# Reordering, re-laying and rewriting the tail of a one-token attention and gated-MLP kernel

## The chip, the cores and the metric

The kernel runs on one core of a Trainium2 chip. The time is device microseconds of one execution, the median of several. The profile is a trace of one execution; its span (first to last recorded instruction) is about 2 us shorter than the time (685.6 against 687.48 us in the profiled run of the kernel before).

Engines in the profile's lines: PE is TensorE's matmul, PEld its weight load, DVE is VectorE, ACT is ScalarE, POOL is GpSimd, SPq is the SyncE queue that issues the DMA transfers.

## The reference, cut to what matters

One decoding step for 4 sequences. The caches hold 32 heads of 4096 keys and values of 128 numbers in bf16: 134 MB each, and all of it is read once.

```python
mod = (silu(c) @ w_mod)                       # six modulation vectors of 512
h = layernorm(x) * (1 + ca) + sa
x = x + ga * attention(h, k_cache, v_cache, wq, wo)
h = layernorm(x) * (1 + cb) + sb
z = gelu_tanh(h @ w_in)                       # 4 x 1792, split in z1 and z2 of 896
g = w_sp * layernorm(z2) + b_sp               # w_sp and b_sp are one number each here
x = x + gb * ((z1 * g) @ w_out)
```

## The kernel before: the parts that matter

The caches are read in 32 tiles each (4 heads of one sequence, 4 MB), on one DMA queue, in the order K, V, K, V; the last key tile comes in two pieces and the last value tile in four. `w_in` and `w_out` are issued behind the last value tile. Scores of a tile are a VectorE product and 16 PE matmuls for each half; `fold` and `softmax` turn them into probabilities, `values` multiplies them with the value tile (128 matmuls of 4 columns), `project` normalises and, after every fourth tile, multiplies with `wo`.

```python
def load_v(i):
    return load(A_v_cache, i, "vt", 4 if i == len(quads) - 1 else 1)   # number of equal pieces

for i in range(NQ + 1):                    # NQ = 32
    ...                                    # loads, query projections, scores(i, 0)
    if i > 1:
        project(i - 2)
    if i > 0:
        fold(i - 1, 1)
        softmax(i - 1)
    if i < NQ:
        scores(i, 1)
        fold(i, 0)
    if i > 0:
        values(i - 1, 0)
        values(i - 1, 1)
project(NQ - 1)
...
nc.sync.dma_start(out=win, in_=B_w_in.rearrange("(j p) n -> p j n", p=P))
nc.sync.dma_start(out=wout, in_=B_w_out.rearrange("(p j) n -> p j n", j=JF))
...                                        # x1, second layernorm -> h2T
for s in range(2):
    for jf in range(JF):
        for j in range(J):
            nc.tensor.matmul(
                z_ps[:, s, jf, :], lhsT=win[:, j, s * FH + jf:(s + 1) * FH:JF],  # every 7th column
                rhs=h2T[:, j, :], start=(j == 0), stop=(j == J - 1),
            )
...   # GELU as copy, 3 steps, exp on ScalarE, add, reciprocal, two products: z1, z2
mean, rstd = ln_stats(post, psum_s, z2b, mean_f, JF, "ln3")
...   # gt = (z2 - mean) * rstd * w_sp + b_sp; uT = gt * z1
...   # y_ps = uT times w_out, 28 matmuls of 4 columns; y = y_ps * modT[5]; yo = y + x1
```

## Time and profile before

| | before |
|---|---|
| time, median | 687.32 us (687.23 to 687.5, 4 runs) |
| span of the profile | 685.6 us |
| read from HBM | 282.73 MB |
| next-to-last value tile landed | 654.28 us |
| span left after that | 31.3 us |

The page's slice view of the kernel before cuts the span in 40 slices of 17 us; a digit is a tenth of busy time (9 is 90% or more), the row GB/s is what the DMA engines moved.

```profile
span 685.6 us, 12370 instructions
...
PEclk9985887777777777777787777777777767776965
DMA  9999999999999999999999999999999999999980
GB/s 368 427 425 429 427 425 425 429 427 431 435 414 428 432 435 426 427 426 427 432 421 430 426 431 435 418 431 429 434 435 420 428 431 435 427 425 418 431 327 12
...
```

The DMA engines are busy from the first slice to the 38th. So the time up to there is set by the transfers, and the change, which leaves the loop as it is, can only shorten the last 30 us.

The chain of waits of the kernel before, from the issue of the next-to-last value tile (columns: start in us, length in us, what):

```profile
...
620.90 33.38 DMA vt<-in_A_v_cache_dram
...
654.32 3.42 PE zo_ps L283 x128
...
657.76 0.19 DVE rz L294
...
658.15 0.60 DVE S L246
...
660.15 0.59 ACT P L267 x2
...
661.97 0.59 ACT P L267 x2
...
663.19 3.43 PE zo_ps L283 x128
...
667.07 0.30 PE attn_ps L302 x6
667.37 1.47 issue
668.84 0.44 PE attn_ps L302 x10
...
672.61 3.13 PE zf_ps L375 x56
...
675.76 0.23 DVE z L380
...
678.35 0.69 PE small L132 x2
...
681.07 0.90 PE y_ps L408 x28
...
682.20 0.21 DVE yo L415
...
```

Two things are to be seen. The last softmax (658.15 to 662.5) begins only after the values of tile 30 (654.32 to 657.74) and their normalisation (`rz`, `oT`), though its scores were done at 653.1: `project(30)` stands before `fold(31, 1)` in VectorE's order. And from 667.37 to 668.84 PE waits for nothing that the profile can name ("issue"), between the sixth and the seventh of 16 matmuls. From 672.61 on `w_in`, the GELU steps, the statistics and `w_out` follow each other with no overlap.

Lines of the timeline of the kernel before (start, length, engine, line, operation, operands, count, and in brackets the idle time before it and what ended it):

```profile
...
667.07 0.30 PE L302 MATMUL attn_ps<-oT,wo_g 128*128 128x4 bf16 x6 [0.47 <-DVE oT L295]
...
668.84 0.42 PE L302 MATMUL attn_ps<-oT,wo_g 128*128 128x4 bf16 x10 [1.47 <-issue]
...
672.58 3.06 PEld L375 LDWEIGHTS <-wt 128*128 128x128 bf16 x56 [2.07 <-issue]
672.61 3.12 PE L375 MATMUL zf_ps<-h2T,wt 128*128 128x4 bf16 x56 [1.96 <-DVE h2T L369]
...
```

The 56 weight loads for `w_in` take 3.06 us, and PE follows at that pace: 56 ns a matmul. The DMA records of the trace show a packet of 16384 bytes on the instruction queue from 666.23 to 667.31 us.

### The profile page before, as it was taken

How to read it: one execution, taken by the hardware profiler on the slowest of the kernel's cores; microseconds unless marked ns; L12 is line 12 of the kernel's file. 1: busy time of each engine (PE TensorE's matmuls, PEld its weight loads, DVE VectorE, ACT ScalarE, POOL GpSimd, SP SyncE). 2: the span in 40 equal slices, each digit the busy share in tenths (PEclk: the TensorE clock that was granted, in tenths of full speed). 3: DMA queues.
4: the chain of work that ended last, by engine and by line, in shares of the span. 5: the costliest groups of instructions: out<-in, count | busy, mean ns of one | idle time of the engine just before them, and what ended most of it. 6: DMA issues, size and time to landing. Idle time of an engine off the chain costs nothing.

```text
span 685.6 us, 12370 instructions
## 1 busy us (share of the span) xinstructions
PE 428.9 (63%) x5696; PEld 249.4 (36%) x5696; DVE 370.7 (54%) x407; ACT 82.7 (12%) x277; POOL 3.6 (1%) x17
## 2 busy tenths in 40 slices
PE   2675856765666666557766455676655577665853
PEld 1241433432334323334433233443333344333443
DVE  2835555466652666445566645546664455665713
ACT  1012101111110111101111100111110011111110
POOL 2000000000000000000000000000000000000000
PEclk9985887777777777777787777777777767776965
DMA  9999999999999999999999999999999999999980
GB/s 368 427 425 429 427 425 425 429 427 431 435 414 428 432 435 426 427 426 427 432 421 430 426 431 435 418 431 429 434 435 420 428 431 435 427 425 418 431 327 12
DMA packets 16963, 283.52 MB, mean 414 GB/s; under 512 B 1416, under 2 KB 6032, under 8 KB 8208
## 3 DMA queue, kind: packets, MB, share of 16 engines
q1 hardware_dynamic: 16832, 282.73, 96.9%
q8 instruction: 44, 0.72, 0.4%
q14 instruction: 7, 0.06, 0.0%
q0 software_dynamic: 64, 0.00, 0.0%
q10 hardware_dynamic: 16, 0.01, 0.0%
HBM read 282.73 MB, written 0.00 MB: 412 GB/s over the span
## 4 chain that ended last, share of the span: by engine, by line
DMA 62%; DVE 21%; PE 15%; issue 1%; ACT 1%; SPq 0%; DVEq 0%; ACTq 0%
DMA kt<-in_A_k_cache_dram 57%; DVE kt L232 17%; PE s_ps L237 12%; DMA vt<-in_A_v_cache_dram 5%; PE zo_ps L283 1%; DVE S L246 1%; DVE mx L254 1%; PE zf_ps L375 0%; DVE mT L256 0%; DVE nm L264 0%; DVE hm L258 0%; ACT P L267 0%; DVE hb L260 0%; DVE oT L295 0%; PE attn_ps L302 0%
## 5 line engine op out<-in xcount | busy, mean ns | idle before, releaser
L237 PE MATMUL s_ps<-kt,ident 128*128 128x512 bf16 x1024 | 294.2, 453 | 224.2 <-DVE kt L232 224.2
L232 DVE TENSOR_TENSOR kt<-kt,qbc 128x8192 bf16<-128x8192 bf16 x64 | 281.8, 4404 | 259.1 <-DMA kt<-in_A_k_cache_dram 259.1
L237 PEld LDWEIGHTS <-ident 128*128 128x128 bf16 x1024 | 115.3, 113 | 389.6 <-issue 247.9
L267 ACT ACTIVATE P<-S,nm 32x128 bf16<-32x128 f32 x128 | 73.9, 577 | 537.3 <-DVE nm L264 534.7
L283 PEld LDWEIGHTS <-vt 128*128 128x128 bf16 x4096 | 108.7, 97 | 1.2 <-DMA vt<-in_A_v_cache_dram 1.2
L283 PE MATMUL zo_ps<-P,vt 128*128 128x4 bf16 x4096 | 108.1, 164 | 1.1 <-DMA vt<-in_A_v_cache_dram 1.1
L246 DVE TENSOR_REDUCE S<-s_ps 128x64 f32<-128x512 f32 x64 | 43.6, 682 | 1.4 <-PE s_ps L237 1.3
L267 ACT ACTIVATION_READ_ACCUMULATOR P<-S,nm 32x1 f32 x128 | 32.1, 251 | 0.0
L278 PEld LDWEIGHTS zo_ps<-rs,ones_f 128*128 128x128 f32 x64 | 12.3, 194 | 9.4 <-ACT P L267 5.0
L185 PE MATMUL big<-wt,hbc 128*32 128x384 bf16 (+1 forms) x128 | 12.2, 525 | 4.2 <-ACT qbc L330 3.7
L294 DVE RECIPROCAL rz<-zo_ps 128x4 f32<-128x4 f32 x32 | 5.6, 175 | 14.3 <-PE zo_ps L283 14.3
L278 PE MATMUL zo_ps<-rs,ones_f 128*128 128x4 f32 x64 | 9.3, 216 | 4.9 <-ACT P L267 4.9
L185 PEld LDWEIGHTS <-hbc 128*32 128x32 bf16 x192 | 6.1, 124 | 13.5 <-issue 10.1
L254 DVE TENSOR_REDUCE mx<-S 128x1 f32<-128x128 f32 x32 | 9.2, 286 | 1.3
L264 DVE STREAM_TRANSPOSE nm<-hb 128x32 f32<-128x32 f32 x32 | 6.8, 212 | 3.2
L330 ACT CAST qbc<-big 128x384 bf16<-128x384 f32 (+1 forms) x8 | 4.3, 532 | 32.7 <-PE big L185 32.7
L256 DVE STREAM_TRANSPOSE mT<-mx 128x32 f32<-128x32 f32 x32 | 6.8, 212 | 1.1
L258 DVE TENSOR_REDUCE hm<-mT 128x1 f32<-128x32 f32 x32 | 5.9, 186 | 1.1
L260 DVE TENSOR_SCALAR hb<-hm 128x32 f32<-128x32 f32 x32 | 5.8, 181 | 1.1
L295 DVE TENSOR_TENSOR oT<-zo_ps,rz 128x4 bf16<-128x4 f32 x32 | 5.4, 168 | 1.1
L302 PEld LDWEIGHTS <-wo_g 128*128 128x128 bf16 x128 | 4.5, 97 | 3.7 <-issue 2.1
L302 PE MATMUL attn_ps<-oT,wo_g 128*128 128x4 bf16 x128 | 4.5, 165 | 1.9 <-issue 1.5
(83 smaller groups left out, 39.9 us busy)
## 6 DMA issues: line engine op xcount, KB each, us to landing
kt<-in_A_k_cache_dram SPq DMA_DIRECT2D x31, 4096.0 KB, 25.6
vt<-in_A_v_cache_dram SPq DMA_DIRECT2D x31, 4096.0 KB, 33.4
wo_g<-in_A_wo_dram SPq DMA_DIRECT2D x8, 512.0 KB, 25.4
kt<-in_A_k_cache_dram SPq DMA_DIRECT2D x2, 2048.0 KB, 23.9
vt<-in_A_v_cache_dram SPq DMA_DIRECT2D x4, 1024.0 KB, 17.3
wt<-in_A_wq_dram SPq DMA_DIRECT2D x1, 3584.0 KB
wt<-in_w_mod_dram SPq DMA_DIRECT2D x1, 2048.0 KB, 36.8
wt<-in_B_w_in_dram SPq DMA_DIRECT2D x1, 1792.0 KB
```

The source lines that it names most:

```text
L185: nc.tensor.matmul(qp[hl * R:(hl + 1) * R, col:col + n], lhsT=hbc[:, j, b, :], rhs=wv[:, g0 - hl0:g0 - hl0 + n, hl, :], start=(j == 0), st ...
L232: nc.vector.tensor_tensor(out=kt, in0=kt, in1=q[:, None, :].to_broadcast([P, HT, DH]), op=ALU.mult,)
L237: nc.tensor.matmul(ps, lhsT=ident, rhs=kt[:, :, cc * DC:(cc + 1) * DC], start=(cc == 0), stop=(cc == DH // DC - 1),)
L246: nc.vector.tensor_reduce(out=st["S", i][:, half * HT:(half + 1) * HT], in_=st.pop(("s", i, half)), axis=AX.X, op=ALU.add,)
L254: nc.vector.tensor_reduce(out=mx[:, 0:1], in_=S, axis=AX.X, op=ALU.max)
L256: nc.vector.transpose(out=mT, in_=mx)
L258: nc.vector.tensor_reduce(out=hm, in_=mT, axis=AX.X, op=ALU.max)
L264: nc.vector.transpose(out=nm, in_=hb)
L267: nc.scalar.activation(out=P4[rows, :, hl], in_=S[rows, :], func=AF.Exp, bias=nm[rows, 0:1], scale=att_scale, accum_out=rs4[rows, hl:hl + 1],)
L278: nc.tensor.matmul(st["z", i], lhsT=ones_f, rhs=rs4s[i % NB], start=True, stop=True,)
L283: nc.tensor.matmul(o_ps, lhsT=st["v", i][:, n, :], rhs=P4[:, n, :], start=(n == 0), stop=(n == NT - 1),)
L302: nc.tensor.matmul(attn_ps[:, jo, :], lhsT=wo_g[:, hl, jo * P:(jo + 1) * P], rhs=oT[:, hl, :], start=(g == 0 and hl == 0 and jo == 0), sto ...
```

## The change

The intent: shorten the tail. (1) For the last tile, fold and softmax go ahead of the projection of tile 30. (2) The last value tile comes in 1/2, 1/4, 1/8, 1/8, so that little work is left behind the last piece. (3) The hidden features are numbered so that the 128 columns of a `w_in` weight load are contiguous; `w_out` is then read in rows of 1024 bytes rather than 7168. (4) GELU becomes one ScalarE function, read straight from PSUM, with table loads placed by hand; the z2 half of `w_in` is multiplied first, into a PSUM tile of its own, so that its GELU can start while PE works on the z1 half. (5) `w_out` multiplies the pair (z1\*z2, z1), before mean and rstd of z2 are known; they are applied to the result, since (z1\*((z2 - mean)\*rstd\*w + b)) @ w_out is w\*rstd\*((z1\*z2) @ w_out - mean\*(z1 @ w_out)) + b\*(z1 @ w_out). (6) The tile name `small` in PSUM gets one buffer instead of two. (7) A helper `keep_busy` is added, but emits nothing.

```diff
-        return load(A_v_cache, i, "vt", 4 if i == len(quads) - 1 else 1)
+        return load(A_v_cache, i, "vt", (2, 4, 8, 8) if i == len(quads) - 1 else (1,))
...
-        ps = psum.tile([P, 2, n, B], F32, name="small", bufs=2)       # and in four more places
+        ps = psum.tile([P, 2, n, B], F32, name="small", bufs=1)
...
-            if i > 1:
+            if 1 < i < NQ:
                 project(i - 2)
             if i > 0:
                 fold(i - 1, 1)
                 softmax(i - 1)
+            if i == NQ:
+                project(i - 2)
...
-        nc.sync.dma_start(out=wout, in_=B_w_out.rearrange("(p j) n -> p j n", j=JF))
+        nc.sync.dma_start(out=wout, in_=B_w_out.rearrange("(j p) n -> p j n", p=P))
...
         mean, rstd = ln_stats(post, psum_s, x1b, mean_d, J, "ln2")
+        nc.scalar.preload_act_table_set("gelu_apprx_tanh_and_others")
+        keep_busy(32)                                                  # empty
...
-        for s in range(2):
+        z_ps = [psum.tile([P, JF, B], F32, name=f"zf{s}_ps") for s in range(2)]
+        for s in (1, 0):
...
-                        z_ps[:, s, jf, :], lhsT=win[:, j, s * FH + jf:(s + 1) * FH:JF],
+                        z_ps[s][:, jf, :], lhsT=win[:, j, s * FH + jf * P:s * FH + (jf + 1) * P],
...
-        (nine steps of GELU; mean, rstd; gt; uT)
+        nc.scalar.activation(out=z2, in_=z_ps[1], func=AF.Gelu_apprx_tanh)
+        u = post.tile([P, JF, 2, B], BF16, name="u")
+        nc.scalar.activation(out=u[:, :, 1, :], in_=z_ps[0], func=AF.Gelu_apprx_tanh)
+        nc.scalar.preload_act_table_set("natural_log_exp_and_others")
+        mean, rstd = ln_stats(post, psum_s, z2b, mean_f, JF, "ln3", lambda:
+            nc.vector.tensor_tensor(out=u[:, :, 0, :], in0=u[:, :, 1, :], in1=z2, op=ALU.mult))
...
-                    y_ps[:, jo, :], lhsT=wout[:, jf, jo * P:(jo + 1) * P], rhs=uT[:, jf, :],
+                    y_ps[:, jo], lhsT=wout[:, jf, jo * P:(jo + 1) * P], rhs=u[:, jf],
...
-        (y = y_ps * modT[5]; yo = y + x1)
+        (yg = y_ps * modT[5]; q = (yg0 - yg1 * mean) * w_sp * rstd; r1 = yg1 * b_sp + x1; yo = q + r1)
```

More of the change, by code (lines that the diff above doesn't have):

```diff
@@ L52 @@
     LN_EPS = 1e-5
-    GK = 0.7978845608028654
     consts = ctx.enter_context(tc.tile_pool(name="consts", bufs=1))
@@ L82, in kv_view, with load @@
         return cache[b, g * NH:(g + 1) * NH].rearrange("h (s n) d -> (h s) (n d)", s=R)
-    def load(cache, i, tag, pieces):
+    def load(cache, i, tag, parts):
         t = kvp.tile([P, NT * DH], BF16, name=tag, bufs=2)
-        w = NT * DH // pieces
-        for k in range(pieces):
-            nc.sync.dma_start(
-                out=t[:, k * w:(k + 1) * w], in_=kv_view(cache, i)[:, k * w:(k + 1) * w],
-            )
+        a = 0
+        for part in parts:
+            b = a + NT * DH // part
+            nc.sync.dma_start(out=t[:, a:b], in_=kv_view(cache, i)[:, a:b])
+            a = b
         return t.rearrange("p (n d) -> p n d", d=DH)
     def load_k(i):
-        return load(A_k_cache, i, "kt", 2 if i == len(quads) - 1 else 1)
+        return load(A_k_cache, i, "kt", (2, 2) if i == len(quads) - 1 else (1,))
     def load_v(i):
-        return load(A_v_cache, i, "vt", 4 if i == len(quads) - 1 else 1)
+        return load(A_v_cache, i, "vt", (2, 4, 8, 8) if i == len(quads) - 1 else (1,))
+    NQ = len(quads)
     ident = consts.tile([P, P], BF16, name="ident")
@@ L111, with keep_busy @@
     nc.vector.memset(eps, LN_EPS)
+    busy_ps = [None]
+    def keep_busy(n):
+        if False:
+            busy_ps[0] = psum_s.tile([P, P], F32, name="busy", bufs=1)
+        for _ in range(0):
+            nc.tensor.matmul(busy_ps[0], lhsT=ident, rhs=ident, start=True, stop=True)
     NB = 3
@@ L126, in bc, with ln_stats @@
         return col[:, None, :].to_broadcast([P, n, B])
-    def ln_stats(pool, psum, buf, ones, n, name):
+    def ln_stats(pool, psum, buf, ones, n, name, meanwhile=None):
         nc.vector.tensor_tensor(out=buf[:, 1], in0=buf[:, 0], in1=buf[:, 0], op=ALU.mult)
-        ps = psum.tile([P, 2, n, B], F32, name="small", bufs=2)
+        ps = psum.tile([P, 2, n, B], F32, name="small", bufs=1)
         nc.tensor.matmul(
@@ L135, in ln_stats @@
         )
+        if meanwhile is not None:
+            meanwhile()
         st = pool.tile([P, 2, B], F32, name=f"st_{name}")
@@ L166, in mod_part @@
     def mod_part(wt, w0, oc):
-        ps = psum_s.tile([P, J, B], F32, name="small", bufs=2)
+        ps = psum_s.tile([P, J, B], F32, name="small", bufs=1)
         for jo in range(J):
@@ L192 @@
     with tc.tile_pool(name="pre", bufs=1) as pre:
-        xc_ps = psum_s.tile([P, J, 2 * B], F32, name="small", bufs=2)
+        xc_ps = psum_s.tile([P, J, 2 * B], F32, name="small", bufs=1)
         for j in range(J):
@@ L219 @@
             nc.scalar.copy(out=qbc[:, b, 0, :], in_=qp[:, b, :])
-        wb_ps = psum_s.tile([P, 2], F32, name="small", bufs=2)
+        wb_ps = psum_s.tile([P, 2], F32, name="small", bufs=1)
         nc.tensor.matmul(wb_ps, lhsT=ones_b, rhs=wb_t, start=True, stop=True)
@@ L282, in values @@
             for n in range(half * HT, (half + 1) * HT):
+                if i == NQ - 1 and n in (NT // 2, 3 * NT // 4, 7 * NT // 8):
+                    keep_busy(NT // 8)
                 nc.tensor.matmul(
@@ L307, in project @@
                         )
-        NQ = len(quads)
         wo_v = A_wo.rearrange("(h p) n -> p h n", p=P)
@@ L369 @@
         nc.vector.tensor_tensor(out=h2T, in0=h2, in1=modT[:, 3], op=ALU.add)
-        z_ps = psum.tile([P, 2, JF, B], F32, name="zf_ps")
-        for s in range(2):
+        z_ps = [psum.tile([P, JF, B], F32, name=f"zf{s}_ps") for s in range(2)]
+        for s in (1, 0):
             for jf in range(JF):
@@ L375 @@
                     nc.tensor.matmul(
-                        z_ps[:, s, jf, :], lhsT=win[:, j, s * FH + jf:(s + 1) * FH:JF],
+                        z_ps[s][:, jf, :], lhsT=win[:, j, s * FH + jf * P:s * FH + (jf + 1) * P],
                         rhs=h2T[:, j, :], start=(j == 0), stop=(j == J - 1),
                     )
-        z = post.tile([P, 2, JF, B], F32, name="z")
-        nc.vector.tensor_copy(out=z, in_=z_ps)
-        zz = post.tile([P, 2, JF, B], F32, name="zz")
-        nc.vector.tensor_tensor(out=zz, in0=z, in1=z, op=ALU.mult)
@@ L383 @@
-        nc.vector.tensor_scalar(
-            out=zz, in0=zz, scalar1=2.0 * GK * 0.044715, scalar2=2.0 * GK,
-            op0=ALU.mult, op1=ALU.add,
-        )
-        nc.vector.tensor_tensor(out=zz, in0=zz, in1=z, op=ALU.mult)
-        nc.scalar.activation(out=zz, in_=zz, func=AF.Exp, scale=-1.0)
-        nc.vector.tensor_scalar_add(out=zz, in0=zz, scalar1=1.0)
-        nc.vector.reciprocal(out=zz, in_=zz)
-        z1 = post.tile([P, JF, B], F32, name="z1")
-        nc.vector.tensor_tensor(out=z1, in0=zz[:, 0], in1=z[:, 0], op=ALU.mult)
+        keep_busy(12)
@@ L393 @@
         z2b = post.tile([P, 2, JF, B], F32, name="z2b")
         z2 = z2b[:, 0]
-        nc.vector.tensor_tensor(out=z2, in0=zz[:, 1], in1=z[:, 1], op=ALU.mult)
-        mean, rstd = ln_stats(post, psum_s, z2b, mean_f, JF, "ln3")
-        gt = post.tile([P, JF, B], F32, name="gt")
-        nc.vector.tensor_tensor(out=gt, in0=z2, in1=bc(mean, JF), op=ALU.subtract)
-        nc.vector.tensor_tensor(out=gt, in0=gt, in1=bc(rstd, JF), op=ALU.mult)
-        nc.vector.tensor_scalar(
-            out=gt, in0=gt, scalar1=wbf[:, 0:1], scalar2=wbf[:, 1:2], op0=ALU.mult, op1=ALU.add,
-        )
@@ L403 @@
-        uT = post.tile([P, JF, B], BF16, name="uT")
-        nc.vector.tensor_tensor(out=uT, in0=gt, in1=z1, op=ALU.mult)
-        y_ps = psum.tile([P, J, B], F32, name="y_ps")
+        nc.scalar.activation(out=z2, in_=z_ps[1], func=AF.Gelu_apprx_tanh)
[4 more added lines that the diff above has]
+            nc.vector.tensor_tensor(out=u[:, :, 0, :], in0=u[:, :, 1, :], in1=z2, op=ALU.mult))
@@ L406 @@
+        y_ps = psum.tile([P, J, 2, B], F32, name="y_ps")
         for jo in range(J):
@@ L408 @@
                 nc.tensor.matmul(
-                    y_ps[:, jo, :], lhsT=wout[:, jf, jo * P:(jo + 1) * P], rhs=uT[:, jf, :],
+                    y_ps[:, jo], lhsT=wout[:, jf, jo * P:(jo + 1) * P], rhs=u[:, jf],
                     start=(jf == 0), stop=(jf == JF - 1),
                 )
-        y = post.tile([P, J, B], F32, name="y")
-        nc.vector.tensor_tensor(out=y, in0=y_ps, in1=modT[:, 5], op=ALU.mult)
+        yg = post.tile([P, J, 2, B], F32, name="yg")
+        nc.vector.tensor_tensor(
+            out=yg, in0=y_ps, in1=modT[:, 5, :, None, :].to_broadcast([P, J, 2, B]), op=ALU.mult,
+        )
+        q = post.tile([P, J, B], F32, name="q")
+        nc.vector.tensor_tensor(out=q, in0=yg[:, :, 1], in1=bc(mean, J), op=ALU.mult)
+        nc.vector.tensor_tensor(out=q, in0=yg[:, :, 0], in1=q, op=ALU.subtract)
+        r1 = post.tile([P, J, B], F32, name="r1")
+        nc.vector.scalar_tensor_tensor(
+            out=r1, in0=yg[:, :, 1], scalar=wbf[:, 1:2], in1=x1, op0=ALU.mult, op1=ALU.add,
+        )
+        nc.vector.scalar_tensor_tensor(
+            out=q, in0=q, scalar=wbf[:, 0:1], in1=bc(rstd, J), op0=ALU.mult, op1=ALU.mult,
+        )
         yo = post.tile([P, B, J], BF16, name="yo")
-        nc.vector.tensor_tensor(out=yo.rearrange("p b j -> p j b"), in0=y, in1=x1, op=ALU.add)
+        nc.vector.tensor_tensor(out=yo.rearrange("p b j -> p j b"), in0=q, in1=r1, op=ALU.add)
         t_ps = psum.tile([J * B, P], F32, name="t_ps")
```

## The prediction

> What bounds the kernel. DMA. The slice view shows DMA at 9 tenths or more for 38 of 40 slices and 425 to 435 GB/s; the page counts 282.73 MB read. The diff alters nothing in the loop over 32 tiles: the instruction order of VectorE, ScalarE and SyncE is the same up to the last tile. So only the tail can pay: from 654.28 us (next-to-last value tile landed) to 685.57 us, 31 us of a 685.6 us span.
>
> The tail before, from the chain of waits and the timeline. 654.32 values of tile 30, 3.42 us on PE; then on VectorE the reciprocal and product of tile 30 and only behind them the last fold and softmax (658.15 to 660.07), since they stand in that order; four exponentials to 662.55; values of tile 31, 663.19 to 666.61; projection with a PE gap of 1.47 us at 667.37 ended by "issue", in which a 16384-byte packet of the instruction queue runs (666.23 to 667.31); second layernorm; 56 matmuls on w_in 672.61 to 675.74 (56 ns each, weight loads 152 ns, against 27 ns and 96 to 104 ns where weights are contiguous); GELU in nine small steps; third layernorm; w_out; output. yo ends at 682.41.
>
> What the change does.
> 1. Fold and softmax of tile 31 go before the projection of tile 30. Its scores end at 653.1, so the exponentials end near 657.7, and PE could go straight on. But the last value tile then binds: by the landings in the trace its quarters land at 656.8, 659.3, 661.8, 664.3. Pieces of 1/2, 1/4, 1/8, 1/8 leave 16 matmuls (0.43 us) after 664.3. Values end at about 664.9, gain 1.7 us, not the 5 us that the order alone promises.
> 2. PE waits for pieces meanwhile[...]. The 1.47 us gap should shrink by about 1 us.
> 3. Contiguous w_in columns: 56 matmuls in about 1.6 us instead of 3.13; the price, 1024-byte rows of w_out, lands perhaps 0.4 us later (46 ns a packet against 275 ns for 7168 bytes) and isn't waited for.
> 4. GELU: seven VectorE steps and an exponential (675.76 to 678.1) become two ScalarE activations of about 0.23 us. The w_out product moves ahead of the layernorm statistics. Two table loads are added, 1.28 us each by the load at the start of this trace. The first hides under h2 and w_in; the second lies between the second GELU and the logarithm and is critical: about 1.3 us[...].
> From the first w_in matmul to the end of yo: 9.80 us before; 4.5 to 6.0 us after, my middle 5.2.
> 5. "small" with one buffer instead of two makes the start serial, about 0.7 us, under the 3.3 us that VectorE waits for the first key tile: free. keep_busy emits nothing.
>
> Sum: 1.7 + 1.0 + (9.8 - 5.2) = 7.3 us. I predict 680.1 us, range 678.6 to 682.0. Faster by over 2% (below 673.6) has chance 0.01, within 2% 0.98, slower 0.01.
>
> Signs. Right if: values of tile 31 wait for DMA and end near 664.9; the "issue" gap in the projection is under 0.7 us; w_in matmuls last under 1.9 us; a table load ends the wait of the last logarithm; yo ends near 675. Wrong if: values(31) still wait for ScalarE; a new instruction-fetch gap opens in w_in or w_out; the table switch costs over 2 us; w_out lands after about 672.5; or the DMA stream itself ends later than 671.

The sum stands, 1.7 + 1.0 + 4.6 = 7.3 us, but the 1.0 us of step 2 stands as the author's estimate. The 9.8 us in the sum is measured; the middle of 5.2 us and the range up to 6.0 are estimates.

## More of the kernel before

PE's granted clock is half of full speed at the end (0.50 in every 5 us stretch from 660 us on).

## The result

| | before | after |
|---|---|---|
| time, median | 687.37 us (687.18 to 687.67, 12 runs) | 678.78 us (678.56 to 678.88, 8 runs) |
| span of the profile | 685.6 | 676.7 |
| next-to-last value tile landed | 654.28 | 654.29 |
| last values end | 666.61 | 664.87 |
| first `w_in` matmul | 672.61 | 669.25 |
| `yo` ends | 682.41 | 673.49 |

The ratio is 0.9874 (95% interval 0.9864 to 0.9884). A ratio here is the mean time of one kernel's fast runs over that of the other's fast runs of the same rounds, so not quite the ratio of the medians quoted. The time fell by 8.6 us or 1.3%, inside the predicted range, 0.2 us from its fast end.

The page's slice view of the kernel after:

```profile
span 676.7 us, 12367 instructions
...
PEclk9985878865678676887667777766787767678885
DMA  9999999999999999999999999999999999999993
GB/s 372 419 417 431 433 429 421 432 431 432 431 421 416 434 431 432 425 426 425 431 431 425 433 432 428 426 423 430 433 430 423 429 427 431 431 426 425 431 410 143
...
```

The loop is as it was; the last slice now still has DMA traffic (143 GB/s), because the kernel ends soon after the last transfer. The chain of waits of the kernel after, in its last part:

```profile
...
644.07 20.16 DMA vt<-in_A_v_cache_dram
...
664.28 0.60 PE zo_ps L297 x16
...
665.34 0.58 PE attn_ps L316 x16
...
669.25 1.63 PE zf_ps L393 x56
670.88 0.51 PE small L142 x2
671.39 0.90 PE y_ps L411 x28
...
672.31 0.20 DVE yg L416
...
673.03 0.25 DVE q L426
...
673.29 0.20 DVE yo L430
...
```

The first line is now the last value tile itself: DMA binds until 664.23 us. Between the last values and `w_in` no piece called "issue" longer than 0.14 us is left. Lines of the timeline of the kernel after, for the groups shown above, the statistics matmul of the third layernorm and the ScalarE operations around it:

```profile
...
665.34 0.56 PE L316 MATMUL attn_ps<-oT,wo_g 128*128 128x4 bf16 x16 [0.48 <-DVE oT L309]
...
669.22 1.58 PEld L393 LDWEIGHTS <-wt 128*128 128x128 bf16 x56 [2.06 <-DMA wt<-in_B_w_in_dram]
669.25 1.63 PE L393 MATMUL zf_ps<-h2T,wt 128*128 128x4 bf16 x56 [1.96 <-DVE h2T L386]
670.17 0.20 ACT L400 ACTIVATE z2b<-zf_ps 128x28 f32<-128x28 f32 x1 [0.39 <-PE zf_ps L393]
...
670.74 0.65 PE L142 MATMUL small<-z2b,mean_f 128*128 128x56 f32 x2
...
671.13 1.28 ACT L405 ACT_TABLE_LOAD   x1
...
672.42 0.30 ACT L157 ACTIVATE rstd_ln<-var_ln,eps 128x4 f32<-128x4 f32 x1
...
```

The 16 projection matmuls come in one run. The 56 `w_in` weight loads take 1.58 us. The GELU of z2 (670.17) starts before the last `w_in` matmul ends (670.88), and the statistics matmul follows without a wait. The second table load ends at 672.41 and the logarithm (L157) starts at 672.42, so the load does hold it up; but its result is ready at 672.95, and the operation that needs it (`q`, 673.03) comes when VectorE gets to it.

By stage the spans differ by 1.7 us up to the end of the last values, 1.6 us from there to the first `w_in` matmul, 5.6 us from there to the end of `yo`, and nothing after it: 8.9 us together.

### The profile page after: what moved, and what is told of

Read it like the earlier page. It is cut to its first block, busy times and chain, and to the rows that moved or that the text cites. A ratio compares the mean times of both kernels' runs of the same rounds, so it can differ in the third digit from the quotient of the medians.

```text
span 676.7 us, 12367 instructions
## 1 busy us (share of the span) xinstructions
PE 429.6 (63%) x5696; PEld 248.3 (37%) x5696; DVE 369.2 (55%) x400; ACT 85.4 (13%) x280; POOL 3.5 (1%) x17
## 4 chain that ended last, share of the span: by engine, by line
DMA 63%; DVE 25%; PE 11%; issue 1%; SPq 0%; ACT 0%; DVEq 0%
DMA kt<-in_A_k_cache_dram 60%; DVE kt L244 20%; PE s_ps L249 9%; DMA vt<-in_A_v_cache_dram 3%; DVE S L258 1%; DVE mx L266 1%; PE zo_ps L297 1%; DVE mT L268 0%; DVE nm L276 0%; DVE hm L270 0%; DVE hb L272 0%; DVE oT L309 0%; SPq L88 0%; DVE rz L308 0%; PE zf_ps L393 0%
```

## The experiments

Twelve kernels ran, five rounds each, all correct. "Saved" is the median of the kernel before in the same call less the median of the variant. The kernel before measured 687.53, 687.67, 687.37 and 687.42 us in the four calls, with single runs up to 0.7 us from these, so differences below about 0.3 us between calls are not read.

| run | what | time | saved |
|---|---|---|---|
| e1_order | before + new order | 685.35 | 2.2 |
| e2_pieces | before + pieces | 687.46 | 0.1 |
| e3_order_pieces | before + both | 685.32 | 2.2 |
| e10_one_small | both + one buffer for `small` | 684.20 | 3.5 |
| e4_contiguous | before + contiguous `w_in` | 686.19 | 1.3 |
| e5_gelu | before + ScalarE GELU | 685.20 | 2.5 |
| e5_defer | before + deferred layernorm | 686.12 | 1.6 |
| after | the whole change | 678.78 | 8.6 |
| e8_two_small | after, two buffers for `small` | 679.75 | 7.9 |
| e11_one_more | e8 + one tiny matmul twice | 678.52 | 8.9 |
| e7_keep_busy | after, `keep_busy` on | 682.89 | 4.5 |
| e9_eight_engines | after, four value tiles split 112+8+8 | 769.19 | -81.8 |
| e12_tail | after, meant to be faster | 678.61 | 8.8 |

The four parts (e10, e4, e5_gelu, e5_defer) add up to 8.8 us, the whole change saves 8.6 us: within what the calls resolve, the gain is accounted for. The traces say a little more. In the stretch from the first `w_in` matmul to the end of `yo`, e4 saves 1.5 us, e5_gelu 2.1 and e5_defer 1.4, together 5.0 of the 5.6 us by which the kernel after is shorter there. The other 0.5 us agrees with what only the whole change has, the z2 half multiplied first: the wait of 0.51 us before the statistics matmul, still there in e5_gelu, is gone. No run isolates it.

### Order and pieces

```diff
# e1_order, on the kernel before
-            if i > 1:
+            if 1 < i < NQ:
                 project(i - 2)
             ...
+            if i == NQ:
+                project(i - 2)
# e2_pieces, on the kernel before: "vt", 4 -> (2, 4, 8, 8)
# e3_order_pieces: both
```

> The kernel before, with only the last fold and softmax moved ahead of the projection of tile 30; the last value tile stays in four equal pieces. Theory A (the order lets PE reach the last values early, then DMA binds): the matmuls on the last value tile wait for its quarters and end near 665.3 us instead of 666.6 (last quarter lands at 664.3, 32 matmuls of 27 ns plus 0.15 us), so 1.3 us; and [...] the 1.5 us gap in the projection goes. Together about 2.8 us, 684.5 us. Rival B (the gap in the projection depends on something else, such as fewer words on the DMA queue or the smaller pieces): the gap of 1.5 us stays and only 1.3 us is won, 686.0 us. Rival C (the order alone is worth its 5 us): 682 us.

> The kernel before, with only the last value tile cut in 1/2, 1/4, 1/8, 1/8 instead of quarters. Theory A: nothing is won, since the last values start at 663.2 us after the exponentials and reach the last piece after it has landed (664.3); values end at 666.6, the gap of 1.5 us in the projection stays; 687.3 us, within 0.3 of before. Rival D (the smaller pieces themselves, landing sooner, are what helped): 0.5 to 2 us faster.

> The kernel before, with order and pieces together. Theory A: values end at 664.9 us, gap gone, 0.4 us faster than the order alone: 3.2 us faster than before, 684.1 us. Rival B: 1.7 us faster, 685.6 us.

PE's lines in the timeline of e1_order:

```profile
...
660.44 2.56 PE L283 MATMUL zo_ps<-P,vt 128*128 128x4 bf16 x90 [2.04 <-issue]
664.37 1.01 PE L283 MATMUL zo_ps<-P,vt 128*128 128x4 bf16 x32 [1.37 <-DMA vt<-in_A_v_cache_dram]
665.86 0.30 PE L302 MATMUL attn_ps<-oT,wo_g 128*128 128x4 bf16 x6 [0.47 <-DVE oT L295]
666.63 0.42 PE L302 MATMUL attn_ps<-oT,wo_g 128*128 128x4 bf16 x10 [0.47 <-issue]
...
```

With the new order the last 32 value matmuls wait for DMA (664.37; the last quarter landed at 664.32) and end at 665.38. That is 1.2 us earlier than before, not the 5 us that the order alone promises: rival C falls, DMA binds. The smaller pieces alone save nothing, as expected: in e2 the last values start at 663.6, when the pieces are nearly all there. In e3 the last values end at 665.05, 0.3 us earlier than in e1, but the time is the same (685.32 against 685.35 us), since the gap in the projection is 0.3 us longer.

The gap in the projection was expected to go in e1 and e3. It shrank to 0.47 us and 0.74 us, and did not go. A second gap of the same kind (2.0 us in e1, 0.9 us in e3) shows between the sixth and seventh value matmul, exactly 128 matmuls (256 PE instructions with their weight loads; a "block" in the expectations of e10 and e11 is this distance) earlier, where the later wait for DMA (1.37 us in e1, 0.67 us in e3) swallows it. So the gap belongs to a place in the instruction stream. In the kernel before, e1, e2 and e3 PE goes on 2.4 to 2.6 us after the start of the packet on the instruction queue (666.23 to 668.84, 664.00 to 666.63, 666.74 to 669.16, 664.15 to 666.56), and the same holds for the earlier gap (658.01 to 660.44 in e1, 658.05 to 660.64 in e3). The gap is that time less what PE still had to do. Theory A was right about the values, only partly right about the gap.

### The single buffer

In the kernel after, the packets on the instruction queue come at 653.57, 660.72 and 667.74 us; in the kernel before and in e1, e2, e3 they come at about 658, 664 to 667, and 671 to 674 us. What else in the change could move them? One buffer for `small` makes the first statistics matmul wait for two engines, and the built program has one more semaphore instruction on PE for it: 11408 PE instructions instead of 11407 (the trace of the kernel after has it at 7.53 us). Every later PE instruction stands one place further in the stream.

```diff
# e8_two_small, on the kernel after; e10_one_small is the reverse, on e3
-        ps = psum.tile([P, 2, n, B], F32, name="small", bufs=1)       # five places
+        ps = psum.tile([P, 2, n, B], F32, name="small", bufs=2)
# e11_one_more, on e8: two PE instructions more near the start, same buffers
         nc.tensor.matmul(wb_ps, lhsT=ones_b, rhs=wb_t, start=True, stop=True)
+        nc.tensor.matmul(wb_ps, lhsT=ones_b, rhs=wb_t, start=True, stop=True)
```

Theory H of the next three expectations is that this place decides. "Fetches" are the starts of the packets on the instruction queue.

> The kernel after, with the small PSUM tiles double-buffered again as before. This takes away one semaphore instruction of PE near the start (11407 instructions in place of 11408)[...]. Theory H [...]: the fetches come at about 658 and 664 us as in the run with order and pieces, a gap of 0.5 to 0.8 us is back in the projection, 679.4 us. Rival I (the gap went for another reason, and one buffer only saves PSUM): 678.8 us, no gap.

> The kernel before with order and pieces, and also one buffer for the small PSUM tiles, which adds the one PE instruction. Theory H: instruction blocks are fetched at about 653.6 and 660.7 us, there is no gap in the projection, 0.7 us faster than order and pieces alone: 684.6 us. Rival I: the gap of 0.74 us stays, 685.3 us.

> The kernel of the double-buffered run, with one tiny matmul near the start issued twice: two PE instructions more, nothing else. Theory H (the offset of the block boundaries counts, not the buffer): the next-to-last fetches come early again (about 653.6 and 660.7 us), the gap of 1.16 us in the projection is gone, 678.8 us. Rival J (the single PSUM buffer and its waits closed the gap, by another way than the count): the gap stays, 679.7 us.

The projection in the timeline of e8_two_small:

```profile
...
665.23 0.30 PE L316 MATMUL attn_ps<-oT,wo_g 128*128 128x4 bf16 x6 [0.48 <-DVE oT L309]
666.68 0.42 PE L316 MATMUL attn_ps<-oT,wo_g 128*128 128x4 bf16 x10 [1.16 <-issue]
...
```

and of e10_one_small, where all 16 matmuls come in one line without an "issue" gap:

```profile
...
665.16 0.56 PE L302 MATMUL attn_ps<-oT,wo_g 128*128 128x4 bf16 x16 [0.47 <-DVE oT L295]
...
```

Undoing the single buffer brings the gap back (1.16 us) and costs 0.7 to 1.0 us (by the column "saved" or by the times); adding it to e3 takes the gap away and saves 1.1 to 1.3 us (684.20 against 685.32 us); and with two buffers but one redundant matmul the gap is gone again (678.52 us, 16 matmuls in 0.56 us). The packets come at 657.93 and 664.15 in e8, at 653.14 and 660.55 in e10, at 652.95 and 660.84 in e11. So the place in the instruction stream decides, not the buffer: rivals I and J fall. All eight profiled kernels without a further PE instruction ahead of the tail (before, e1, e2, e3, e4, both e5, e8) show the late packets; the five with one or two more (after, e7, e10, e11, e12) show the early ones; e9, whose stream of tiles ran at another pace, is left out. Why a shift of one or two places makes the first of these packets come 4.4 to 5.0 us earlier (653.57 in the kernel after and 652.95 in e11 against 657.93 in e8; 653.14 in e10 against 658.05 in e3), while PE stands waiting for value tile 30, the records don't show; that stays open.

### Contiguous weights

```diff
# e4_contiguous, on the kernel before
-        nc.sync.dma_start(out=wout, in_=B_w_out.rearrange("(p j) n -> p j n", j=JF))
+        nc.sync.dma_start(out=wout, in_=B_w_out.rearrange("(j p) n -> p j n", p=P))
-                        z_ps[:, s, jf, :], lhsT=win[:, j, s * FH + jf:(s + 1) * FH:JF],
+                        z_ps[:, s, jf, :], lhsT=win[:, j, s * FH + jf * P:s * FH + (jf + 1) * P],
```

> The kernel before, with only the feature order of the hidden layer changed, so that the w_in columns of one weight load are contiguous and w_out is read in rows of 1024 bytes. Theory A: the 56 w_in matmuls take 1.6 us instead of 3.13, all of it on the critical path: 1.5 us faster, 685.8 us; w_out lands about 0.3 us later, unnoticed. Rival E (the time of w_in is set by the granted clock of 0.5 or by the arrival of w_in, not by the stride): no gain.

The `w_in` lines in the timeline of e4_contiguous:

```profile
...
672.71 1.58 PEld L375 LDWEIGHTS <-wt 128*128 128x128 bf16 x56 [2.07 <-issue]
672.74 1.63 PE L375 MATMUL zf_ps<-h2T,wt 128*128 128x4 bf16 x56 [1.97 <-DVE h2T L369]
...
```

The 56 weight loads take 1.58 us instead of 3.06, 104 ns each instead of 152, and the kernel saves 1.3 us. The granted clock there is 0.50 in the kernel before and in the kernel after, whose 56 loads take 1.58 us too. Rival E falls: the stride was the cost. `w_out` landed at 671.23 us in this run, against 670.89 in the kernel before, and nobody waited for it.

### GELU and the table loads, and the deferred layernorm

```diff
# e5_gelu, on the kernel before
         mean, rstd = ln_stats(post, psum_s, x1b, mean_d, J, "ln2")
+        nc.scalar.preload_act_table_set("gelu_apprx_tanh_and_others")
...
-        (nine steps of GELU)
+        nc.scalar.activation(out=z2, in_=z_ps[:, 1], func=AF.Gelu_apprx_tanh)
+        nc.scalar.activation(out=z1, in_=z_ps[:, 0], func=AF.Gelu_apprx_tanh)
+        nc.scalar.preload_act_table_set("natural_log_exp_and_others")
# e5_defer, on the kernel before: old GELU; y_ps from the pair (z1*z2, z1), then yg, q, r1, yo as in the change
```

> The kernel before, with only the GELU changed: two ScalarE GELU activations straight from PSUM and two table loads in place of seven VectorE steps and an exponential. Theory A (a table load costs its 1.28 us on ScalarE and hides behind the statistics): z2 is ready 0.25 us after the last w_in matmul instead of 2.3; 2.1 us faster, 685.4 us; the logarithm waits for the load by at most 0.2 us. [...]

> The kernel before, with only the layernorm of the gate deferred: w_out multiplies the pair z1*z2 and z1 (8 columns a matmul), and mean and rstd are applied to its result. The old GELU stays; one small VectorE copy is added to fill the pair. Theory A: from the start of the statistics matmul to the end of yo 2.8 us instead of 4.06: 1.2 us faster, 686.3 us. Rival G (the six VectorE steps after w_out eat what the two steps fewer ahead of it give): within 0.4 us of before.

Lines of the timeline of e5_gelu around the second table load:

```profile
...
676.15 1.28 ACT L385 ACT_TABLE_LOAD   x1
...
677.49 0.16 DVE L143 TENSOR_TENSOR var_ln<-st_ln,msq_ln 128x4 f32<-128x4 f32 x1
...
677.68 0.30 ACT L145 ACTIVATE rstd_ln<-var_ln,eps 128x4 f32<-128x4 f32 x1 [0.24 <-DVE var_ln L143]
...
```

The load ends at 677.43, the variance that the logarithm needs at 677.65, the logarithm starts at 677.68: the table load costs nothing here. From the last `w_in` matmul to the statistics matmul it takes 0.51 us instead of 2.61, which is the 2.1 us expected; the measured 2.5 us is 0.4 us more, which the trace does not show. A load takes 1.28 us in each record of before, after and e5_gelu, and no further cost shows around it: in the kernel after the logarithm starts 0.01 us after a load that it was waiting for, and both loads start 0.02 us after the ScalarE operation before them.

In e5_defer the stretch from the start of the statistics matmul to the end of `yo` takes 2.62 us instead of 4.06, and 1.6 us is saved. Rival G falls: the steps after `w_out` that replace the old ones are paid for by the 0.9 us of `w_out` matmuls and the 0.5 us of logarithm and exponential that now run side by side.

### keep_busy switched on

```diff
# e7_keep_busy, on the kernel after
-        if False:
+        if busy_ps[0] is None:
             busy_ps[0] = psum_s.tile([P, P], F32, name="busy", bufs=1)
-        for _ in range(0):
+        for _ in range(n):
```

> The kernel after with its empty keep_busy switched on: 80 extra 128x128 matmuls in the tail that nothing reads. Theory N (they only stand in PE's way: 32 of them between the second layernorm and w_in and 12 between w_in and the statistics, at 60 to 110 ns each): 0.5 to 2 us slower, 680 us, granted clock in the tail still 0.5. Rival O (they keep the granted clock of TensorE at 1 and so shorten the last matmuls, 0.6 us to 0.3 us each for the fp32 pairs): 678 us or faster.

It is 4.1 us slower than the kernel after, twice the most that I had allowed. The trace counts 92 extra matmuls, not 80, and the expectation costed only 44 of them. The 48 between the pieces of the last value tile were what it missed: each block of 16 holds PE for about 1.65 us (660.99 to 662.65, at the granted clock of 0.5; 104 ns a matmul, within the 60 to 110 allowed), and the last values end at 667.94 instead of 664.87. The block of 12 makes the stretch from the first `w_in` matmul to the statistics matmul 2.77 us instead of 1.49. Rival O is right for one stretch: the granted clock from 665 to 670 us is 0.74 instead of 0.50, and the fp32 statistics matmul of the second layernorm (two PE records) takes 0.38 us instead of 0.60. From 660 to 665 us it stays 0.50 though PE is busy all the time, and that of the third takes 0.62 us instead of 0.65. So it wins tenths of a microsecond and stands in the way for whole ones.

### The lag between the completions of a tile

```diff
# e9_eight_engines, on the kernel after
+        if tag == "vt" and 16 <= i < 20:
+            for r0, r1 in ((0, 112), (112, 120), (120, 128)):
+                nc.sync.dma_start(out=t[r0:r1], in_=kv_view(cache, i)[r0:r1])
+            parts = ()
```

> The kernel after, with four value tiles (16 to 19) read as 112 partitions and twice 8 partitions. [...] In the trace of after, 8 of the 16 completions of a tile come 8 to 10 us later than the other 8 by the end, a lag that grows from 1 us at the start. Theory K [...]: the 16 completions of the last tiles come within 3 us, the last value piece lands 4 to 5 us earlier, 674.5 us, faster than both kernels. Rival L [...]: the lag doubles to 18 us and the kernel ends 4 to 5 us later, 683.5 us. Rival M [...]: no change, 678.8 us.

The reason to try it: in the trace of after the 16 completions of value tile 30 spread over 9.6 us, in two groups of eight (644.7 to 647.9 and 652.6 to 654.3 us), and the last group is what PE waits for. In order of landing the later eight come 6.4 to 7.9 us behind the earlier eight, a little less than the expectation says. For the key tile that landed at 28.30 us the 16 completions spread over 1.9 us.

This one failed in a way that no theory named: 769 us (six runs, 766.3 to 776.8). The stretches of e9_eight_engines before and during the split tiles (columns: stretch, its length, busy us and counts of the engines, granted clock, DMA share, GB/s):

```profile
...
300.00:360.00 60.00, 38.14 (x485) 21.63 (x483) 33.86 (x33) 6.94 (x24) 0.00 (x0) 0.72 1.01 425
360.00:520.00 160.00, 48.13 (x553) 26.49 (x551) 44.86 (x44) 9.25 (x32) 0.00 (x0) 0.59 1.00 211
...
```

and of the kernel after in the second of these stretches:

```profile
...
360.00:520.00 160.00, 102.66 (x1321) 58.80 (x1319) 90.21 (x88) 18.55 (x64) 0.00 (x0) 0.73 1.00 429
...
```

The DMA engines stay busy but move 211 GB/s instead of 429: a packet of 32 KB, 1.215 us in the kernel after, takes 2.3 to 2.5 us at the median in most of this stretch, those of untouched key tiles too. Why, no run here shows. So whether the lag can be moved stays open, and so does which engines lag: the records don't name them.

### A version meant to beat both

```diff
# e12_tail, on the kernel after
-        return load(A_v_cache, i, "vt", (2, 4, 8, 8) if i == len(quads) - 1 else (1,))
+        return load(A_v_cache, i, "vt", (2, 4, 8, 16, 16) if i == len(quads) - 1 else (1,))
...
-        nc.vector.tensor_tensor(out=h2, in0=h2, in1=bc(rstd, J), op=ALU.mult)
         nc.vector.tensor_tensor(out=h2, in0=h2, in1=modT[:, 4], op=ALU.mult)
+        nc.vector.tensor_tensor(out=h2, in0=h2, in1=bc(rstd, J), op=ALU.mult)
```

> A version meant to beat both: the kernel after, with the multiplication by the modulation put ahead of the one by rstd in the second layernorm (so it runs while ScalarE still computes rstd), and the last value tile cut in 1/2, 1/4, 1/8, 1/16, 1/16. If the tail is one chain as the profile of after has it: values end 0.2 us earlier (8 matmuls of 27 ns behind the last piece instead of 16), the second layernorm ends 0.2 us earlier, the first w_in matmul starts at about 668.85 us, just behind the landing of w_in at 668.7; 678.4 us, 0.4 us faster than after. If the arrival of w_in or of w_out binds from there (w_out landed at 671.1, first used at 671.4): 0 to 0.3 us.

The last piece landed at 664.46 us in this run, 0.23 later than in the kernel after, and still the first `w_in` matmul starts 0.19 us earlier (669.06): 0.4 us are won up to there. Then the timeline shows the `w_out` weight loads:

```profile
...
671.34 0.82 PEld L411 LDWEIGHTS <-wt 128*128 128x128 bf16 x28 [0.31 <-DMA wt<-in_B_w_out_dram]
671.34 0.91 PE L411 MATMUL y_ps<-u,wt 128*128 128x8 bf16 x28
...
```

They wait for the landing of `w_out` (671.3 us). `yo` ends at 673.46, as in the kernel after. The 0.2 us between 678.61 and 678.78 us are not resolved, so this is no proven improvement: the tail has come within reach of the end of the DMA stream.

## Why the prediction was right, point by point

- Direction, size and range were right: 680.1 us predicted with 678.6 to 682.0, 678.78 us measured, but only just inside: two terms were too small, both in the same direction (steps 2 and 4). The saving was 8.6 us, predicted 7.3. Of the five signs for "right" four came; `yo` ended at 673.5, not near 675. One sign for "wrong" came too, by 0.1 us: the DMA stream ended at 671.12, not by 671, and it cost nothing.
- Step 1, the last value tile binds and the order is worth 1.7 us: right. The last values waited for DMA and ended at 664.87 (predicted 664.9); e1, e2 and e3 show that the order is what pays; the pieces move the end of the values by 0.3 us and, with the gap still there, the time by nothing.
- Step 2, the gap shrinks as "PE waits for pieces meanwhile": size about right (1.0 us predicted, 1.5 us vanished), cause only half right. With PE ahead the packet did come about 2 us earlier in e1 and e3 (664.00 and 664.15 instead of 666.23), but that left 0.47 and 0.74 us of gap in e1 and e3 and 1.16 us in e8. What closed it in the kernel after is one more PE instruction, a by-product of the single buffer, which step 5 had called free. The prediction got this gain partly by luck.
- Step 3, contiguous weights: right, 1.63 us for 56 matmuls (predicted 1.6). `w_out` landed at 671.12 instead of 670.89, 0.2 us later (predicted 0.4); its first weight load starts at 671.16, but its first matmul only at 671.38, behind the statistics matmul, so the landing cost nothing.
- Step 4, from `w_in` to `yo` 5.2 us: this term was mis-sized. It took 4.24 us, below even the low end of 4.5. My middle left room for a larger cost of a table load than its 1.28 us, and called the second load critical. No larger cost showed, and the load held the logarithm up by about 0.4 us (its variance was ready at 672.04) behind VectorE work of the same length, so it cost nothing. The step also left out that the z2 half goes first, which agrees with 0.5 us more.
- Step 5, the serial start: it is free, as predicted (VectorE waits 2.15 us for the first key tile instead of 3.33, so 1.2 us longer to get there, predicted 0.7); the next-to-last value tile landed at 654.29 us instead of 654.28.
- The sum: 1.7 + 1.6 + 5.6 us by the trace against 1.7 + 1.0 + 4.6 us predicted.

## What to carry to other kernels

In a kernel bound by DMA, ask of a reorder what lands last: the order here freed PE 5 us earlier (657.65 in e1 against 662.60 us, the matmuls behind the last exponentials), and the last values ended 1.2 us earlier, because the data came then (664.32 us). Lay out weights so that the columns of one weight load are contiguous (1.58 against 3.06 us here), and apply per-column factors behind a matmul so that it need not wait for their statistics (1.6 us saved in e5_defer). A gap that ends in "issue", with a packet on the instruction queue 2.4 to 2.6 us before its end, belonged here to a place in the instruction stream; try one instruction more or less before it, and don't credit whatever change happened to move it.
